# Two more steps of a top-k attention kernel transpose their weights on TensorE, and one pair is dealt fewer products

## The chip, the cores and the metric

The kernel runs on one core of one Trainium2 chip. The metric is device time in microseconds (us) of one execution, lower is better. The time before is the median of three executions, 1654.76 us (1654.59 to 1656.15). One further execution, taken by the hardware profiler, lasted 1655.26 us; its span from first to last instruction is 1653.4 us.

## What is computed

Attention that keeps the 32 largest scores of each row, then a low-rank token mixer and a two-layer channel network:

```python
# q, k, v: 8 batches x 8 heads x 576 rows x 64, float32
scores = scale * q @ k.T
kth    = 32nd largest of each row of scores
attn   = softmax(where(scores >= kth, scores, -1e9))
x      = (attn @ v), heads side by side          # 8 x 576 x 512
u      = x + (x.T @ U @ V).T                     # rank 32
out    = u + relu(u @ w_ch1) @ w_ch2             # 512 -> 2048 -> 512
```

## The kernel before

**Tiling.** Two heads form a *pair*, four pairs a batch: pairs 0 to 31, in the code `g`. The 576 rows of a pair are four tiles of 128 rows (t = 0 to 3) and a tail of 64 (t = 4, both heads in one tile). A *step* is one (g, t); from pair 4 on the tail goes together with t = 3, so a pair has four steps. The second batch is pairs 4 to 7, and its third pair is pair 6. The loop over steps is at the end of the kernel; step number n = 20 is (4, 0), n = 28 is (6, 0).

**What a step does.** TensorE makes the scores (L350, tail L382), ScalarE copies them out of PSUM (L395, tail L415 and L418). From pair 5 on, the two halves of a row are folded: GpSimd adds them (L446), VectorE takes their maximum (L448), GpSimd subtracts it (L449); then VectorE searches for the 32 largest with alternating MAX8 and MATCH_REPLACE8 (L500, L502, L521, L534, L539). L502 opens a step's search and needs L449. The threshold goes to ScalarE (L565, L571), GpSimd subtracts the gap (L572), ScalarE takes the exponential (L453). The resulting weights must be transposed before they can be multiplied with v (L708, L711, tail L682; copied out at L720).

**Two ways to transpose.** `turns` does it on TensorE: nine 128x128 transposes per step (L634 eight times, L639 once) into PSUM, through a ring of two buffers named tp, and three ScalarE copies into PT (L635 twice, L640). `blocks` does it on VectorE: three stream transposes of 32x32 blocks (L598) into y, four DMAs from SyncE's queue that write y to DRAM (L604), and later, in `back`, one DMA on ScalarE's queue that reads it all into PT (L613). `shared(g, t)` says which: when it is true, `blocks` is called at the end of the step's follower and `turns` returns at once. The tail always goes through TensorE.

**Products dealt between the steps.** The two layers of the previous batch's channel network are a generator of matmuls (L845 the first layer, L862 the second), called in small portions by `fill`, eight times a step. One unit is a matmul of 512 columns; a batch has 144 units, and a portion is 144/(4 x 8 x 4.4) = 1.023 units, times 1.4 in a pair's last step. In pairs 4 to 7 and the first three steps of pair 8 the portion is multiplied by EARLY, one factor a pair (the last one also in those three steps). What isn't done in time is done later: the next batch's network can't start before its input is complete, and waits (`yield 0`), in which case the portion lapses. Every engine takes its instructions in the order in which this loop has emitted them.

**Other names.** L750, L761, L773, L781, L785, L800 and L801 belong to the low-rank mixer (`mixed`), L873, L874, L886, L888 and L890 to the way of the network's output back to DRAM, L857 to the first layer's activation. VectorE's L320 transposes the next pair's q and k, which SyncE's queue loads (L272, L277). L938 is the last batch's network, with its own scheme. ACT is ScalarE, DVE VectorE, POOL GpSimd.

Of the kernel before, what the change touches and what calls it, by code (L numbers as in the profile page):

```python
# [26 lines left out]
def kernel(  # L27
# [35 lines left out]
    NT, TAIL = 4, 64  # L63
# [8 lines left out]
    ROUNDED = NPAIR + 2  # L72
# [512 lines left out]
    def shared(g, t):  # L585


        return t < NT and g >= ROUNDED

    def blocks(g, t):  # L590

# [26 lines left out]
    def turns(g, t):  # L618


        if shared(g, t):
            return
        E2 = probs.pop((g, t))
        nh = 2 if t < NT else 1
        if t == NT and g >= NPAIR:
            PT = attn.tile([P, NT + 1, P], F32, tag="PTt", name="PTt", bufs=1)
        else:
            PT = attn.tile([P, 2 * NT + 1, P], F32, tag="PT", name="PT")
        PTs[g, t] = PT
        for h in range(nh):  # L630
            tp = ps_t.tile([P, NT, P], F32, tag="tp", name="tp")
            for j in range(NT):
                a = h * (S + TAIL) + j * P
                nc.tensor.transpose(tp[:, j, :], E2[:, a : a + P], ident)  # L634
            nc.scalar.copy(PT[:, NT * h : NT * h + NT], tp)  # L635
            yield
        tp = ps_t.tile([P, P], F32, tag="tp", name="tp")
        a = MAIN if nh == 2 else S - P
        nc.tensor.transpose(tp, E2[:, a : a + P], ident)  # L639
        nc.scalar.copy(PT[:, NT * nh], tp)  # L640
        yield
# [31 lines left out]
    def values(g, t):  # L673
# [31 lines left out]
        if shared(g, t):  # L705
            PT = PT.rearrange("p c n -> p (c n)")
            PT = PT.rearrange("p (a c j) -> p c a j", a=4, j=BLK)
# [452 lines left out]
    BATCH = NPAIR * NT  # L1160


    SLOTS, LONG, EARLY = 8, 1.4, (1.1, 0.75, 0.91, 0.95)
    share = MLP_WORK / (NPAIR * SLOTS * (NT - 1 + LONG))
    fillers, mixing, due = [], [], 0.0

# [48 lines left out]
    t = 0  # L1215
# [5 lines left out]
    for n in range(STEPS + 2):  # L1221
        if n < STEPS:
            g, t = steps[n][0]
# [8 lines left out]
        else:  # L1232
            t = NT
# [109 lines left out]
        for tile_ in tiles(n - 1):  # L1343
            if shared(*tile_):
                blocks(*tile_)
# [50 lines left out]
```

## Time and profile before

| what | value |
|---|---|
| median of three runs | 1654.76 us |
| the profiled execution | 1655.26 us |
| its span | 1653.4 us |
| mean granted TensorE clock | 0.971 |
| L598, stream transpose of 128x512 | 208 times, 681 ns mean |
| L598, stream transpose of 128x128 | 104 times, 269 ns mean |
| L635, copy of 128x512 to PT | 52 times, 600 ns mean |
| L640, copy of 128x128 to PT | 28 times, 271 ns mean |
| L845 and L862, products | 1792 records each, two a matmul |

TensorE's ends are modelled, so that its busy share says little; starts are what counts, and a float32 product leaves two records. A time such as 312.86 is in us from the span's start. In a timeline a row gives start, duration, engine, line, operation, tiles and count, and in brackets the engine's idle time before it with what ended it. In a table of windows the columns are the stretch, its length, then the busy us and the instructions of TensorE, its weight loads, VectorE, ScalarE and GpSimd, the granted TensorE clock, the busy share of the DMA engines, and GB/s.

### The profile page before, as it was taken

What the parts mean: (1) busy time and instruction counts of PE and PEld (TensorE: products, weight loads), DVE (VectorE), ACT (ScalarE), POOL (GpSimd) and SP (SyncE); (2) the same over time, 40 slices, a digit from 0 to 9 for tenths busy, and PEclk for the clock granted to TensorE, in tenths of its full rate; (3) what the DMA queues carried; (4) which work ended last, traced back from release to release, by engine and by line L of the source; (5) the groups of instructions that cost most, each with busy time, mean ns of one, the idle gap of its engine ahead of it and who ended that gap; (6) DMA issues with size and microseconds to landing.
All of it is one profiled execution on the core that took longest, in us unless ns stands there. A gap on an engine that the chain in (4) does not pass through costs nothing.

```text
span 1653.4 us, 30246 instructions
## 1 busy us (share of the span) xinstructions
PE 1554.9 (94%) x9638; PEld 1182.0 (71%) x9638; DVE 1546.1 (94%) x4394; ACT 990.1 (60%) x2475; POOL 1009.4 (61%) x881
## 2 busy tenths in 40 slices
PE   4566799999899999999999999999999999999998
PEld 2344466787667877788777877788777877788776
DVE  7999999999999999999999999999999999994452
ACT  4888887665556556565656556565656656564320
POOL 4888768656566565656566565656566565653720
PEclk7787899999999999999999999999999999999999
DMA  3333331345445455554545455554545455543001
GB/s 89 102 96 99 88 88 31 84 128 139 132 120 142 127 141 136 143 139 129 134 123 143 125 146 134 143 139 127 135 123 144 126 148 134 139 123 108 7 2 28
DMA packets 280399, 189.42 MB, mean 115 GB/s; under 512 B 174288, under 2 KB 261168, under 8 KB 280240
## 3 DMA queue, kind: packets, MB, share of 16 engines
q1 hardware_dynamic: 259728, 117.62, 29.6%
q10 hardware_dynamic: 20512, 69.87, 13.3%
q8 instruction: 76, 1.25, 0.3%
q14 instruction: 83, 0.68, 0.1%
HBM read 116.49 MB, written 70.91 MB: 113 GB/s over the span
## 4 chain that ended last, share of the span: by engine, by line
PE 69%; DVE 22%; DMA 3%; POOL 2%; SPq 1%; ACT 1%; issue 1%; DVEq 0%; ACTq 0%; POOLq 0%
PE mm L862 21%; PE mm L845 20%; DVE m L539 7%; PE sc L350 6%; DVE upper L534 6%; PE O L711 6%; PE mm L938 3%; DVE first L521 2%; PE tp L938 2%; PE sc L938 2%; PE sc L382 2%; PE up L785 2%; DVE y L598 1%; PE O L708 1%; DVE upper L502 1%; DVE place L534 1%
## 5 line engine op out<-in xcount | busy, mean ns | idle before, releaser
L845 PE MATMUL mm<-uT,w 128*128 128x320 f32 (+1 forms) x1792 | 460.2, 408 | 2.1 <-POOL uT L801 2.1
L862 PE MATMUL mm<-hT,w 128*128 128x320 f32 (+1 forms) x1792 | 460.4, 407 | 0.0
L572 POOL TENSOR_TENSOR Ssb<-Ssb,E 128x576 f32<-128x576 f32 x243 | 339.7, 1417 | 196.9 <-ACT E L571 196.8
L845 PEld LDWEIGHTS mm<-uT,w 128*128 128x128 f32 x1792 | 333.3, 190 | 102.2 <-issue 10.0
L862 PEld LDWEIGHTS mm<-hT,w 128*128 128x128 f32 x1792 | 331.9, 190 | 91.7 <-issue 9.8
L539 DVE MAX8 m<-upper 128x8 f32<-128x304 f32 (+1 forms) x774 | 362.5, 509 | 0.7
L534 DVE MATCH_REPLACE8 upper<-m,upper 128x304 f32<-128x304 f32 (+1 forms) x516 | 256.6, 504 | 0.0
L446 POOL TENSOR_TENSOR lower<-Ssb 128x576 uint32<-128x576 uint32 x108 | 152.3, 1410 | 134.2 <-ACT Ssb L395 66.9
L449 POOL TENSOR_TENSOR lower<-lower,upper 128x576 uint32<-128x576 uint32 x108 | 152.3, 1410 | 123.6 <-DVE upper L448 119.7
L453 ACT ACTIVATE Ssb<-Ssb,nmax 128x576 f32<-128x576 f32 x258 | 201.8, 784 | 19.9 <-POOL Ssb L545 9.6
L350 PE MATMUL sc<-qkT 64*128 64x288 f32 (+1 forms) x1056 | 177.5, 457 | 9.6 <-ACT Ssb L404 8.5
L571 ACT ACTIVATE E<-Ssb,least 128x576 f32<-128x576 f32 x243 | 176.2, 768 | 4.2
L502 DVE MAX8 upper<-lower 128x8 f32<-128x288 f32 x432 | 171.8, 439 | 2.3 <-POOL lower L449 2.3
L395 ACT COPY Ssb<-sc 128x576 f32<-128x576 f32 x216 | 127.6, 642 | 73.5 <-PE sc L350 73.5
L598 DVE STREAM_TRANSPOSE y<-Ssb 128x512 f32<-128x512 f32 (+1 forms) x312 | 154.0, 544 | 0.4 <-ACT Ssb L453 0.4
L711 PE MATMUL O<-PT,va 128*64 128x128 f32 x2048 | 144.1, 284 | 0.0
L857 ACT ACTIVATE hT<-mm 128x320 f32<-128x320 f32 (+1 forms) x224 | 91.2, 407 | 85.0 <-PE mm L845 81.5
L350 PEld LDWEIGHTS sc<-qkT 64*128 64x128 f32 (+1 forms) x1056 | 95.2, 196 | 50.5 <-issue 18.9
L711 PEld LDWEIGHTS O<-PT,va 128*64 128x64 f32 x2048 | 112.6, 140 | 16.2 <-issue 1.6
L720 ACT COPY XT<-O 128x128 f32<-128x128 f32 x128 | 33.8, 264 | 114.3 <-PE O L711 107.3
L534 DVE MATCH_REPLACE8 upper<-first,upper 128x304 f32<-128x304 f32 x216 | 97.5, 459 | 0.0
L500 DVE MATCH_REPLACE8 lower<-upper,lower 128x288 f32<-128x288 f32 x216 | 93.9, 442 | 0.0
(268 smaller groups left out, 2261.1 us busy)
## 6 DMA issues: line engine op xcount, KB each, us to landing
away<-y SPq DMA_DIRECT2D x416, 144.0 KB
PT<-away ACTq DMA_DIRECT2D x104, 576.0 KB
raw<-in_moe_w_ch_dram SPq DMA_DIRECT2D x32, 512.0 KB
va<-in_v_dram SPq DMA_DIRECT2D x64, 128.0 KB
scale<-rd ACTq DMA_DIRECT2D x56, 144.0 KB
out_dram<-ob SPq DMA_DIRECT2D x59, 128.0 KB
ld<-in_q_dram SPq DMA_DIRECT2D x108, 64.0 KB
ld<-in_k_dram SPq DMA_DIRECT2D x108, 64.0 KB
```

Source lines behind the costliest of these rows:

```text
L350: nc.tensor.matmul(out, lhsT=qkT[half(h), 0, cols(t)], rhs=qkT[half(h), 1, lo:hi], start=True, stop=True,)
L446: nc.gpsimd.tensor_tensor(bottom, a.bitcast(U32), b.bitcast(U32), ALU.add)
L453: nc.scalar.activation(E, chunk, AF.Exp, bias=nmax, scale=SCALE, accum_out=total)
L502: nc.vector.max(spot, lower)
L534: nc.vector.match_replace(nxt, ms[c], curs[c], NEG)
L539: nc.vector.max(ms[c], curs[c])
L571: nc.scalar.activation(gap, chunk, AF.Relu, bias=least[:, c : c + 1], scale=-WIDEN)
L572: nc.gpsimd.tensor_tensor(chunk, chunk, gap, ALU.subtract)
L598: nc.vector.transpose(y[:, :, i * NT : i * NT + c].rearrange("p r c j -> p c r j"), E2[:, a : a + c * P].rearrange("p (c r j) -> p c r j", ...
L711: nc.tensor.matmul(O[half(h)], lhsT=va[:, h, j, :], rhs=PT[:, NT * h + j], start=False, stop=(j == NT - 1),)
L845: nc.tensor.matmul(phs[f][:, 0:w], lhsT=first_layer(cc, f), rhs=uT[:, cc, lo:hi], start=(cc == 0), stop=(cc == NC - 1),)
L862: nc.tensor.matmul(po[:, 0:w], lhsT=w2[:, f, c * P : (c + 1) * P], rhs=hTs[f][:, 0:w], start=(f == 0), stop=(f == NF - 1),)
```

## The change

The predicate now sends the first two steps of pair 6 to TensorE as well, and pair 6 is dealt fewer products, pair 7 and the three steps after it slightly more:

```diff
     def shared(g, t):
-        return t < NT and g >= ROUNDED
+        return t < NT and (g, t) >= (ROUNDED, NT // 2)
...
-    SLOTS, LONG, EARLY = 8, 1.4, (1.1, 0.75, 0.91, 0.95)
+    SLOTS, LONG, EARLY = 8, 1.4, (1.1, 0.75, 0.78, 0.97)
     share = MLP_WORK / (NPAIR * SLOTS * (NT - 1 + LONG))
```

ROUNDED is 6 and NT is 4, so the comparison starts at (6, 2). The places at which the loop asks `shared`, and the two functions it chooses between, are unchanged:

```python
        for tile_ in tiles(n - 1):
            if shared(*tile_):
                blocks(*tile_)
        turning = turned(n - 1)
...
    def turns(g, t):
        if shared(g, t):
            return
```

In the order in which the built program's instructions stand, L598 occurs 306 times after, 312 before; L634 336 times after, 320 before; L639 58 times after, 56 before; L845 and L862 896 times each in both. The orders differ from pair 6's first steps until the step that follows the scores of (8, 3), and are the same from there to the end.

## The prediction

> **What bounds the kernel now.** I read the page's busy shares and chain first, then windows, then the timelines of each engine around pair 6.
>
> ```profile
> PE 1554.9 (94%) x9638; PEld 1182.0 (71%) x9638; DVE 1546.1 (94%) x4394; ACT 990.1 (60%) x2475; POOL 1009.4 (61%) x881
> ...
> PE 69%; DVE 22%; DMA 3%; POOL 2%; SPq 1%; ACT 1%; issue 1%; DVEq 0%; ACTq 0%; POOLq 0%
> ```
>
> TensorE and VectorE are both nearly full, and the chain that ended last has both. Where it changes from one to the other decides this case. The windows:
>
> ```profile
> 294.00:341.00 47.00, 46.15 (x315) 36.23 (x311) 44.60 (x137) 30.39 (x81) 28.86 (x25) 1.00 0.32 85
> ...
> 388.00:435.00 47.00, 42.13 (x278) 31.13 (x276) 46.97 (x144) 27.27 (x69) 28.96 (x26) 0.96 0.50 136
> ...
> 575.00:761.40 186.40, 186.27 (x1190) 143.74 (x1189) 185.84 (x565) 112.25 (x285) 115.20 (x100) 1.00 0.51 135
> ```
>
> Pair 6 is the first row: VectorE lacks 2.4 us. In pair 8 VectorE never rests and TensorE lacks 4.9 us. One later batch, the third row, has TensorE full and VectorE with 0.56 us to spare; the next batch repeats it to the record count. So VectorE sets the time up to about 490 us, TensorE after it. The chain says the same: mostly VectorE and the DMAs behind its transposes until 491.10, then TensorE's products almost without a break until 1485. The point of change is a wait for a PT tile:
>
> ```profile
> 491.10 0.49 PE L708 MATMUL O<-PT,vd 128*128 128x128 f32 x2 [1.85 <-DMA PT<-away]
> ```
>
> From 297 to 575 TensorE waited this often:
>
> ```profile
> PE O L708 <- DMA PT<-away: 4.9, 4, 1.9
> PE mm L845 <- POOL uT L801: 2.1, 1, 2.1
> ```
>
> From 575 to 1480 the same query names no wait of TensorE at all. The waits also cost clock:
>
> ```profile
> 413.50:416.90 3.40, 1.70 (x9) 0.86 (x8) 3.40 (x11) 1.16 (x5) 2.41 (x5) 1.00 0.59 191
> 416.90:420.30 3.40, 3.37 (x30) 2.42 (x31) 3.40 (x7) 2.08 (x5) 2.17 (x3) 0.54 0.20 47
> 488.60:492.00 3.40, 1.55 (x13) 0.92 (x13) 3.37 (x12) 2.68 (x7) 2.31 (x3) 1.00 0.52 168
> 492.00:495.40 3.40, 3.40 (x22) 2.04 (x19) 3.40 (x14) 1.22 (x3) 1.88 (x2) 0.54 0.68 175
> ```
>
> After a stretch of 3.4 us in which TensorE was busy for half or less, the next one runs at about half clock: some 1.7 us of TensorE's work lost, twice, the second time on the path.
>
> **What the Trainium skill says.** "TensorE: Matmul & The Clock Gate", Part 1, describes this clock: a free-running window of 3.4 us, half rate after an idle one. The rows above agree, and free-running means that the loss may come or go between runs. Its Part 4 says that a TensorE transpose lands in PSUM and has to be copied out; the trace agrees (L635, L640). "VectorE: DVE Perf Modes", section "The three transpose paths", says that VectorE transposes 32x32 blocks only; here that shows as the detour y, DRAM, PT behind L598.
>
> **The change part by part.**
>
> *Removed from VectorE.* Three L598 for (6, 0) and three for (6, 1). From start to start they take 314.26 - 312.86 = 1.40 and 325.81 - 324.40 = 1.41, together 2.8 us.
>
> ```profile
> 312.86 1.48 DVE L598 STREAM_TRANSPOSE y<-Ssb 128x512 f32<-128x512 f32 x3
> 314.26 0.78 DVE L502 MAX8 upper<-lower 128x8 f32<-128x288 f32 x2
> ...
> 322.08 0.76 DVE L448 TENSOR_TENSOR upper<-sc,Ssb 128x576 f32<-128x576 f32 x1 [1.44 <-ACT Stail L415]
> ...
> 324.40 1.48 DVE L598 STREAM_TRANSPOSE y<-Ssb 128x512 f32<-128x512 f32 x3
> 325.81 1.34 DVE L320 STREAM_TRANSPOSE qkT<-ld 128x1152 f32<-128x1152 f32 x1
> ```
>
> What is late next: at the first place L502, which needs GpSimd's L449. That ran from 311.44 for 1.42, to 312.86, just when VectorE would arrive: a wait of 0 to 0.3, I take 0.05 (in the new order an L874 of 0.87 stands before L449, but L446 ahead of it can start earlier, as ScalarE's L571 no longer stands behind an L873 that waited 1.58 for TensorE). At the second, L320 still covers L449. Eight L604 and two L613 go too; SyncE's loads then stand behind two waits less, worth nothing here.
>
> *The stall at 322.08.* VectorE waited 1.44 for the scores of (6, 3). TensorE had started them (L350) at 319.68; L448 follows 2.4 later. With two products of 320 columns less before the scores of (6, 2) (0.54 each: sixteen records in 4.31) and one product and three L886 (0.33) less between them, these scores start about 1.9 earlier, at 317.8, and L448 can run at 320.2. VectorE would come at 320.64 - 1.35 = 319.3. About 0.9 of the 1.44 stays, 0.5 goes.
>
> *Added to TensorE.* 16 L634 and 2 L639. Their price:
>
> ```profile
> 308.20 1.09 PE L634 MATMUL tp<-ident,Ssb 128*128 128x128 f32 x8
> ```
>
> Eight start within 0.93 (the next product is at 309.13), four in 0.43 in the chain, so 0.11 each and 2.0 us in all. The first nine stand right after the scores of (6, 3), the others after those of (7, 0).
>
> *Dealt products.* Pair 6 loses 0.13 x 36 = 4.7 units; a unit is 0.54 x 512/320 = 0.86 us, so 4.0 us. Pair 7 gets 0.7 units, the three next steps 0.5. The rest, about 2 units, or four products of 256 columns by the new order, runs after the scores of (8, 3), where the portions lapsed before and where TensorE stood idle (408 to 425). It delays nothing there.
>
> *Added to ScalarE.* Two times L635, L635, L640: 0.60 + 0.60 + 0.27 = 1.47 each, 2.9 us on an engine busy for 30.4 of pair 6's 47. They stand in order before an L453. The tp ring has two buffers, and in the new order the first two copies come after L395, L415 and L418, so that an L886 on TensorE waits about 0.5; I take 0.5 for each step, bounds 0 and 1.5.
>
> *Does TensorE keep up?* Against before, the scores start: (6, 3) -1.9, (7, 0) -1.6, (7, 1) -1.2, (7, 2) -1.7 (a wait of 0.63 for L781 goes), (7, 3) -1.3. VectorE is then 2.8 + 0.5 - 0.1 = 3.2 early. The tightest place is (7, 3): ScalarE's copies ended at 366.35 and L448 ran at 368.56, 2.2 of slack, against 1.9 wanted. It just holds; a loss of 0 to 0.8 lies in the range. In pair 8 slack is 3.6 and more, and TensorE's waits there (1.1, 1.4, 0.2 and 2.1, by DMA and L801, which follow VectorE) let it catch up.
>
> *The sum.* VectorE, and with it the DMA that TensorE waits for at 491.10, comes 3.2 us earlier. From there on the order is unchanged and TensorE sets the time, so 3.2 carries to the end. In the likeliest case one more thing goes: TensorE reaches that place with less idle time, or at another phase of the clock's window, and the half-clock stretch at 492.0 or most of the DMA wait isn't met. The first is worth up to 1.7, the second up to 1.8; I take 1.4. VectorE can follow: it stood idle for 0.7 + 0.4 in pair 10 for this same delay, and rests 0.4 a batch later. Sum: 1655.26 - 3.2 - 1.4 = 1650.7. The profiled execution was 0.5 above the median; I compare the forecast with the median as it stands, 4.1 below it.
>
> **The rivals.**
>
> *A, the forecast:* 3.2 and a part of the wait or clock at 490, between 1648.9 (both whole) and 1651.4. Chance 0.57.
>
> *B, only VectorE's part arrives:* TensorE meets the same DMA wait and the same half clock 3 us earlier. For it: both follow VectorE. 1655.26 - 3.2 = 1652.1; with up to 1.3 lost at (7, 3) or 491, 1653.4. Chance 0.26, of which 0.04 ends beyond 0.2%.
>
> *C, nothing arrives:* the transposes' 2.0 us on TensorE aren't covered by idle time but shift the chain after 491, against 3.2 gained: 1654.1, up to 1655.5. Against it: 7.8 us of waits between 297 and 495. Chance 0.09.
>
> *D, slower:* TensorE falls behind in pair 6, because the tp ring is held by copies that stand in ScalarE's order behind waiting ones. If each of the four groups of eight and one waits 1.5 for its copy (6 us), less the 4.0 of products taken out, plus the 2.0 of transposes, TensorE is 4 later at pair 7; the slack there is 2 to 5, so VectorE waits instead of gaining, and a new half-clock window adds 1.7. It decides from about 6 us of ring waits on. 1658.7. Against it: pair 5 transposes all its steps so, and TensorE's waits around them from 250 to 298 add up to 2.2 (0.9, 0.7, 0.4 and 0.2). Chance 0.08.
>
> *That it doesn't do what it says* can be excluded: six L598 fewer, eighteen transposes more, equal products.
>
> **How the numbers follow.** 0.2% is 3.3 us, about what a measurement of this kernel can tell from no change. Faster by more: 0.57 + 0.04 = 0.61. Within: 0.22 + 0.09 = 0.31. Slower: 0.08. The range takes in A and B, 1648.9 to 1653.4, and leaves out C and D.
>
> **What would show it.** No L598 before (6, 2)'s at about 337; L448 of (6, 3) at about 320 with a wait near 0.9; the L502 after it at 323.8 instead of 327.06; VectorE without idle time in pairs 7 to 9; the L708 that started at 491.10 at 488 or earlier; the clock table without, or with, a half-clock stretch after it; batches of 186.4 as before. The prediction is wrong if VectorE stands idle in pair 7, or if TensorE's batches become longer.

## The result and the profile after

The changed kernel takes 1651.49 us (median of 14 runs, 1650.63 to 1654.33), the kernel before in the same comparison 1654.70 us (14 runs, 1653.91 to 1657.64). The ratio is 0.9979, with a 95% interval of 0.9971 to 0.9986: 3.2 us faster. A second comparison on the chip, further down, gives 0.9976 (0.9967 to 0.9984). The two intervals are gains of 2.3 to 4.8 us and 2.6 to 5.5 us. Of all executions timed for this study one, of the spare transposes further down, took 3139.16 us; the ratios leave it out. The forecast was 1650.7, the range 1648.9 to 1653.4.

The profiled execution of the changed kernel took 1653.27 us, more than its median. It lost that time before the change acts: VectorE opened (6, 0) at 296.84 us, not at 294.22 as before. Over all runs of this study that moment lies between 294.2 and 296.8. So I count from VectorE's first L502 of (6, 0) on. From that point to the opening of (9, 0), two executions of one kernel agree within 0.06 us.

First the page's engine row and the shares of its chain, for the changed kernel:

```profile
PE 1558.9 (94%) x9656; PEld 1185.5 (72%) x9656; DVE 1543.5 (93%) x4388; ACT 993.8 (60%) x2481; POOL 1009.1 (61%) x881
...
PE 72%; DVE 13%; POOL 5%; ACT 4%; DMA 2%; SPq 1%; issue 1%; DVEq 0%; ACTq 0%; POOLq 0%
```

Eighteen matmuls more on TensorE and six instructions fewer on VectorE, as the change says. VectorE's share of the chain has gone from 22% to 13%. That does not mean that VectorE is free now. The chain is one path among several of nearly the same length.

The timeline of VectorE in pair 6 shows where the time went:

```profile
306.49 0.82 DVE L502 MAX8 upper<-lower 128x8 f32<-128x288 f32 x2 [0.94 <-POOL lower L449]
...
315.50 0.82 DVE L502 MAX8 upper<-lower 128x8 f32<-128x288 f32 x2
...
322.96 0.76 DVE L448 TENSOR_TENSOR upper<-sc,Ssb 128x576 f32<-128x576 f32 x1 [1.03 <-ACT Stail L415]
...
326.57 0.78 DVE L502 MAX8 upper<-lower 128x8 f32<-128x288 f32 x2
...
340.00 1.48 DVE L598 STREAM_TRANSPOSE y<-Ssb 128x512 f32<-128x512 f32 x3
```

Before, the last two of these rows stood here:

```profile
327.06 0.78 DVE L502 MAX8 upper<-lower 128x8 f32<-128x288 f32 x2
...
340.49 1.48 DVE L598 STREAM_TRANSPOSE y<-Ssb 128x512 f32<-128x512 f32 x3
```

Subtract 2.62 from the rows of the changed kernel to compare with before. The search that began at 314.26 now begins at 312.88, the one at 327.06 at 323.95, and the L598 at 340.49 stands at 337.38. The L502 at 315.50 has no bracket (idle times under 0.15 us get none): GpSimd's L449 is in time. L448 still waits for the scores of (6, 3), for 1.03 us where it was 1.44.

On TensorE the added transposes follow the scores of (6, 3), and those of the next step follow the scores of (7, 0) (rows of the timeline, where one row merges neighbours of a kind):

```profile
320.56 1.24 PE L350 MATMUL sc<-qkT 64*128 64x288 f32 x8
321.74 0.66 PE L634 MATMUL tp<-ident,Ssb 128*128 128x128 f32 x4
322.23 0.71 PE L862 MATMUL mm<-hT,w 128*128 128x320 f32 x2
322.77 0.60 PE L634 MATMUL tp<-ident,Ssb 128*128 128x128 f32 x4
...
324.19 0.33 PE L639 MATMUL tp<-ident,Ssb 128*128 128x128 f32 x1
...
332.62 0.27 PE L761 MATMUL tp<-ident,uT 128*64 128x128 f32 x1 [0.35 <-ACT PT L635]
```

Of the brackets in pair 6, the last one, 0.35 us, is the only new one that a copy out of the tp ring causes. Then the waits of TensorE from 290 to 575 (us in total, times, longest):

```profile
PE mm L845 <- POOL uT L801: 2.1, 1, 2.1
PE tp L634 <- ACT XT L720: 0.9, 1, 0.9
PE O L708 <- DMA PT<-away: 0.6, 2, 0.3
```

The wait of L708 for the DMA was 4.9 and is 0.6. And the place that stood at 491.10, in the timeline, with the two windows of the clock around it below:

```profile
486.71 2.32 PE L862 MATMUL mm<-hT,w 128*128 128x320 f32 x8
488.94 0.49 PE L708 MATMUL O<-PT,vd 128*128 128x128 f32 x2
```

```profile
488.17:491.58 3.41, 3.41 (x31) 2.13 (x29) 3.38 (x12) 2.02 (x5) 2.18 (x2) 1.00 0.28 48
491.58:495.00 3.42, 3.42 (x20) 2.66 (x19) 3.42 (x13) 2.74 (x8) 3.15 (x3) 1.00 0.68 174
```

L708 does not wait, and TensorE's clock stays at 1.00. Counted from (6, 0) it comes at 192.10 instead of 196.88, so 4.8 us earlier.

This table counts from VectorE's first L502 of (6, 0) to that of the steps named; the last column runs to the end of the span:

| kernel | (7,0) | (9,0) | (11,0) | (20,0) | (31,3) | end |
|---|---|---|---|---|---|---|
| before | 47.68 | 140.60 | 234.85 | 653.90 | 1197.31 | 1359.22 |
| before, profiled again | 47.67 | 140.59 | 234.85 | 653.91 | 1197.30 | 1359.08 |
| changed | 44.57 | 137.50 | 230.43 | 648.62 | 1191.84 | 1354.65 |
| changed, profiled again | 44.56 | 137.49 | 230.42 | 648.59 | 1191.75 | 1354.25 |
| transposes alone | 47.72 | 140.65 | 233.58 | 651.84 | 1195.56 | 1357.99 |
| dealing alone | 46.13 | 139.05 | 231.99 | 650.69 | 1194.11 | 1355.91 |
| two later steps too | 44.56 | 137.49 | 230.43 | 649.92 | 1193.33 | 1355.61 |
| spare transposes | 47.67 | 140.60 | 233.53 | 651.72 | 1194.68 | 1357.41 |

The 4.57 us from (6, 0) to the end divide like this. Pair 6 gives 3.11. From (9, 0) to (11, 0) it took 94.25 and takes 92.93, which gives 1.32. From (11, 0) to the end it took 1124.37 and takes 1124.22: nothing more. VectorE's further lead of 1.05 at (31, 3) is gone at the end, to within the 0.7 us by which three profiled executions of the changed kernel differ there (1354.25 to 1354.96).

### The profile page after: what moved, and what is told of

Same layout as the page of the kernel before. It is cut to its first block, busy times and chain, and to the rows that moved or that the text cites. A ratio compares the mean times of both kernels' runs of the same rounds, so it can differ in the third digit from the quotient of the medians.

```text
span 1651.5 us, 30266 instructions
## 1 busy us (share of the span) xinstructions
PE 1558.9 (94%) x9656; PEld 1185.5 (72%) x9656; DVE 1543.5 (93%) x4388; ACT 993.8 (60%) x2481; POOL 1009.1 (61%) x881
## 4 chain that ended last, share of the span: by engine, by line
PE 72%; DVE 13%; POOL 5%; ACT 4%; DMA 2%; SPq 1%; issue 1%; DVEq 0%; ACTq 0%; POOLq 0%
PE mm L862 22%; PE mm L845 21%; PE sc L350 7%; PE O L711 6%; DVE m L539 4%; DVE upper L534 3%; PE mm L938 3%; PE up L785 2%; PE tp L938 2%; PE sc L938 2%; PE sc L382 2%; PE O L708 1%; PE tp L634 1%; DVE first L521 1%; DVE upper L502 1%; POOL E L544 1%
## 5 line engine op out<-in xcount | busy, mean ns | idle before, releaser
L845 PE MATMUL mm<-uT,w 128*128 128x320 f32 (+1 forms) x1792 | 461.1, 408 | 2.6 <-POOL uT L801 2.1
L862 PE MATMUL mm<-hT,w 128*128 128x320 f32 (+1 forms) x1792 | 460.6, 408 | 0.0
L845 PEld LDWEIGHTS mm<-uT,w 128*128 128x128 f32 x1792 | 333.1, 190 | 102.5 <-issue 9.6
L862 PEld LDWEIGHTS mm<-hT,w 128*128 128x128 f32 x1792 | 332.0, 190 | 91.6 <-issue 9.8
L449 POOL TENSOR_TENSOR lower<-lower,upper 128x576 uint32<-128x576 uint32 x108 | 152.4, 1411 | 135.9 <-DVE upper L448 134.0
L502 DVE MAX8 upper<-lower 128x8 f32<-128x288 f32 x432 | 171.8, 438 | 1.7 <-POOL lower L449 1.7
L395 ACT COPY Ssb<-sc 128x576 f32<-128x576 f32 x216 | 127.5, 642 | 72.7 <-PE sc L350 72.6
L598 DVE STREAM_TRANSPOSE y<-Ssb 128x512 f32<-128x512 f32 (+1 forms) x306 | 150.9, 543 | 0.0
```

The costliest lines, as they stand in the source:

```text
L449: nc.gpsimd.tensor_tensor(bottom, bottom, top.bitcast(U32), ALU.subtract)
L502: nc.vector.max(spot, lower)
L845: nc.tensor.matmul(phs[f][:, 0:w], lhsT=first_layer(cc, f), rhs=uT[:, cc, lo:hi], start=(cc == 0), stop=(cc == NC - 1),)
L862: nc.tensor.matmul(po[:, 0:w], lhsT=w2[:, f, c * P : (c + 1) * P], rhs=hTs[f][:, 0:w], start=(f == 0), stop=(f == NF - 1),)
```

## The experiments

**The two parts apart.** Theory: VectorE gains 2.8 us only if TensorE brings the scores earlier, which the smaller dealing does. Rival: one of the two edits is enough. The first kernel has the new predicate and the old dealing, the second the reverse:

```diff
-        return t < NT and g >= ROUNDED
+        return t < NT and (g, t) >= (ROUNDED, NT // 2)
```

> The kernel before with only the two steps' transposes moved to TensorE, the products dealt as before. Measured from VectorE's first L502 of (6, 0) to that of (9, 0): before 140.6 us, the changed kernel 137.5. Theory (both halves are needed): the first L598 that goes is swallowed by the wait for the scores of (6, 3), which grows from 1.44 to about 2.8, because no product was taken from ahead of those scores; of the second, TensorE's 2.0 us of transposes take most back at (7, 3), where slack is 2.2. The stretch is 139.2 to 140.6, the time 0 to 1.4 us under before. Rival (VectorE's work alone counts): 137.8, the time 2.8 under before.

```diff
-    SLOTS, LONG, EARLY = 8, 1.4, (1.1, 0.75, 0.91, 0.95)
+    SLOTS, LONG, EARLY = 8, 1.4, (1.1, 0.75, 0.78, 0.97)
```

> The kernel before with only the new factors 0.78 and 0.97, the transposes where they were. Theory: the wait of 1.44 for the scores of (6, 3) goes, nothing else in pair 6, so the same stretch is 139.2 instead of 140.6, and the time 1.4 us under before, more if the DMA wait at 491 is met in another way. Rival (the dealing is the whole gain, the transposes only move): 137.5 and 3.2 under before.

The transposes alone: 1653.57 us against 1654.40, ratio 0.9996 (0.9988 to 1.0004). The dealing alone: 1653.22 us, 0.9995 (0.9986 to 1.0003). At (9, 0), the first is 0.05 late, the second 1.55 early, both together 3.11 early. The timeline of VectorE in the first kernel shows what became of the six L598:

```profile
318.44 0.85 DVE L539 MAX8 m<-upper 128x8 f32<-128x304 f32 x2
322.05 0.76 DVE L448 TENSOR_TENSOR upper<-sc,Ssb 128x576 f32<-128x576 f32 x1 [2.76 <-ACT Stail L415]
...
327.04 0.82 DVE L502 MAX8 upper<-lower 128x8 f32<-128x288 f32 x2 [1.31 <-POOL lower L449]
```

L448 stands where it stood before (322.08): VectorE came 1.3 earlier and waited 1.3 longer for the scores of (6, 3). The second saving becomes a wait for L449, since L449 needs this L448. So both savings are eaten in pair 6 already. I had expected the second one to go later, at (7, 3). In the changed kernel the scores come earlier: L448 waits 1.03, and the L502 after it has no bracket. The dealing alone gains 1.55 in pair 6, which is about the stall of 1.44. The two parts are worth more together in pair 6 (3.11) than apart (-0.05 + 1.55), so the rival falls for either edit. The times agree as far as they go: neither part alone is clear of no change, the two together are. From (6, 0) to the end, the profiles show more, 1.2 and 3.3 us; 1.3 of each is the matter of pair 10, below.

**Two later steps on TensorE as well.** If TensorE sets the time after 491, the same exchange in pair 16 must cost what TensorE gets, although VectorE is relieved by 2.8 us there. The rival, that VectorE bounds there too, expects a gain.

```diff
-        return t < NT and (g, t) >= (ROUNDED, NT // 2)
+        return t < NT and (g, t) >= (ROUNDED, NT // 2) and (g, t) not in ((16, 0), (16, 1))
```

> The changed kernel with the transposes of (16, 0) and (16, 1) moved to TensorE as well, no product taken out for them. Theory (from about 490 us on TensorE sets the time, without idle time): 18 transposes of 0.11 us are added and the end comes 1 to 2 us later than in the changed kernel; VectorE's 2.8 us turn into idle time of VectorE at the scores of later steps. Rival (VectorE still sets the time there): 2.8 us earlier.

1652.83 us (21 runs), 0.9987 (0.9980 to 0.9994) against before; the changed kernel had 0.9979. From (6, 0), it equals the changed kernel until pair 14 (369.82 against 369.83), is 1.30 later at (20, 0), and 0.96 later at the end (0.65 to 1.36 later than the three profiled executions of the changed kernel). That is less than the 2.0 us that TensorE gets, and just under the 1 to 2 expected; what hides the rest was not traced. VectorE's waits from 250 to 1500, first in the changed kernel and then in this one:

```profile
DVE upper L502 <- POOL lower L449: 1.7, 2, 0.9
DVE upper L448 <- ACT Stail L415: 1.6, 3, 1.0
```

```profile
DVE upper L448 <- ACT Stail L415: 3.0, 5, 1.2
DVE upper L502 <- POOL lower L449: 2.7, 3, 1.0
DVE upper L448 <- ACT Ssb L395: 1.1, 1, 1.1
```

The sums are 3.3 and 6.8: VectorE waits for the scores and folds after them instead of transposing. The transposes alone cost 0.05 us in pair 6, where TensorE has idle time ahead of 491, and the same number of them cost 1.3 us at (20, 0), where it has none. That agrees with the prediction's reading of the windows. Whether fewer products in pair 16 would have changed this was not tried.

**What the 1.3 us at pair 10 are.** Before was profiled again, to see whether its wait at L708 comes back, and a kernel was made that leaves pairs 6 to 10 as before but puts 18 transposes of the identity at step 10, long ahead of them. It puts 18 more matmuls ahead of TensorE's later instructions and so moves the places at which TensorE fetches them. (The spare results go nowhere.)

> The kernel before, unchanged, with another profile. Theory: the start of (6, 0) on VectorE, 293.98 before and 296.60 in the changed kernel, differs between executions of one and the same code by 1 to 3 us, with the half-clock stretches of the first 200 us; the stretch from (6, 0) to (9, 0) is the same within 0.2 (140.6). The DMA wait near 491 and the half-clock stretch after it may or may not come. Rival (these belong to the program): 293.98 again, and both again.

```diff
+        if n == 10:
+            spare_ = ps_t.tile([P, P], F32, tag="tp", name="spare_")
+            for _ in range(18):
+                nc.tensor.transpose(spare_, ident, ident)
```

> The kernel before with 18 more TensorE transposes of the identity, early (step 10 of the loop, where TensorE is idle a third of the time), whose result nobody reads. It moves the places at which TensorE fetches its instructions (one 16 KB packet every 256 of its instructions) by as many instructions as the change does, and touches nothing in pairs 6 to 10. Theory: the wait near 491 comes from such a fetch that falls between the writes to away and the read of PT, 1.5 us of delay; shifted, the PT read is issued 5.5 to 6.0 us after its L598 instead of 7.0, TensorE's gap there is under 0.6 instead of 1.85 to 2.0, VectorE's idle 1.1 in pair 10 goes, and the stretch from the first L502 of (6, 0) to that of (11, 0) is 233.6 as with the transposes alone, instead of 234.85; (9, 0) stays at 140.6. Rival (the wait depends on how early VectorE or how busy TensorE is): 234.85, and the gap again.

> The changed kernel unchanged, with another profile. Theory: the start of (6, 0) lies near 294.4 as in the others and not at 296.84; from it to (9, 0) 137.5, to (11, 0) 230.4, to the end 1354.7, each within 0.3. Rival (the change itself delays the start): 296.8 again.

The single times were 1655.34 (before), 1653.73 (spare transposes) and 1651.39 (changed). Before again: the wait returns, 2.03 us, and so does the half clock after it. Changed again: neither. (6, 0) opened at 294.47 in before and at 295.34 in the changed kernel, so that the 296.84 of its first profile does not belong to it (294.4 had been expected). The spare transposes change nothing until (9, 0) (140.60 as before), and then gain the same 1.32 that the changed kernel gains: from (9, 0) to (11, 0) 92.93. So this part of the gain needs neither pair 6's transposes on TensorE nor its dealing: 18 idle matmuls, long before, do the same.

Its cause can be followed one step back. The trace of before holds 76 packets of 16 KB on a queue of kind "instruction" (and packets of 8 KB on another one, which I leave aside). "Runtime: NRT & Kernel Launch", section "Instruction fetch mechanics", says that each engine fetches its instructions over DMA in blocks of 16 KiB, 256 instructions. The trace agrees for TensorE: from one packet of 16 KB to the next, some 20 us, it records 256 instructions of TensorE on average. In before, one came at 189.9 us from (6, 0), between the last write of L604 (issued at 188.5) and the read L613 (192.7), which needs those writes. With the spare transposes it came at 186.9, ahead of the writes, and in the changed kernel at 183.9, also ahead of them. From the first L598 to the issue of L613 it took 486.92 - 479.89 = 7.03 us in before, 484.93 - 479.40 = 5.53 in the changed kernel (before's two rows come first):

```profile
479.89 1.48 DVE L598 STREAM_TRANSPOSE y<-Ssb 128x512 f32<-128x512 f32 x3
486.92 0.33 ACTq L613 DMA_DIRECT2D PT<-away  x1
```

```profile
479.40 1.48 DVE L598 STREAM_TRANSPOSE y<-Ssb 128x512 f32<-128x512 f32 x3
484.93 0.35 ACTq L613 DMA_DIRECT2D PT<-away  x1
485.33 0.42 ACT L873 COPY oT<-mm 128x320 f32<-128x320 f32 x1 [1.48 <-DMA away<-y]
```

The spare transposes had 6.10, the transposes alone (fetch at 187.5, after the first of their writes) 6.00, the dealing alone, whose fetch at 188.4 fell behind its writes (185.6 to 187.0), 7.1. These agree with a fetch that delays the writes by some 1 to 1.5 us. Two other steps show the same in the kept traces. At (15, 2) a packet falls between the last write and the read in both executions of before and in the dealing alone, 6.88 to 6.99 us from transpose to read; in the ten other executions it doesn't, 5.28 to 5.33. At (9, 0) it is the other way round: the two executions of before have none there, 5.18 and 5.20, and the two of the spare transposes do, 6.72 and 6.95. At later steps the difference is often smaller or absent. No run isolates the fetch from all else that 18 more matmuls shift, so its part remains a reading, though a supported one.

The longer wait alone is not what costs 1.3, and this was not what I had thought. The dealing-alone kernel waits too, for 1.62 us (its timeline), yet it needs 92.94 from (9, 0) to (11, 0), as the changed kernel does. The windows of the clock tell the difference. First before's window that holds the wait and the one after it, then the same for the dealing alone:

```profile
488.85:492.26 3.41, 1.56 (x18) 1.04 (x18) 3.38 (x10) 2.43 (x7) 2.32 (x2) 1.00 0.48 152
492.26:495.68 3.42, 3.42 (x20) 2.06 (x15) 3.42 (x14) 1.50 (x3) 1.62 (x2) 0.50 0.67 172
```

```profile
490.01 0.49 PE L708 MATMUL O<-PT,vd 128*128 128x128 f32 x2 [1.62 <-DMA PT<-away]
```

```profile
487.67:491.08 3.41, 1.79 (x17) 1.14 (x17) 3.38 (x12) 2.69 (x7) 2.41 (x3) 1.00 0.62 169
491.08:494.50 3.42, 3.42 (x28) 2.40 (x24) 3.42 (x13) 2.11 (x5) 2.73 (x3) 1.00 0.68 174
```

TensorE was busy for 1.56 of 3.41 in before and ran at half clock next; in the other kernel it was busy for 1.79 and kept its full clock. Before profiled again had 1.38 and half clock. So the 1.3 us belong to the half-clock stretch, and the wait counts when it empties about half of one window.

**Does that part show in the times?** Three kernels were timed in one comparison: the spare transposes, the changed kernel, and the variant described next.

> The kernel before with the 18 early spare transposes, timed. Theory: the place of TensorE's instruction fetch is worth 1 to 1.7 us at the end in most executions, so the median is 1 to 1.7 us under before although no work was removed; the rest of the changed kernel's gain, 1.5 to 2.5 us, is the transposes and the dealing. Rival (the wait near 491 is rare or costs nothing in most executions): the median of before, within 0.4 us.

> The changed kernel, timed beside the others. Theory: 3.0 to 3.6 us under before; from (6, 0) to (9, 0) 137.5 again.

Before: 1654.74. The changed kernel: 1651.07, ratio 0.9976 (0.9967 to 0.9984). The spare transposes: 1654.29, ratio 1.0000 (0.9992 to 1.0008), so the 1 to 1.7 us that I expected did not show, although their profiled execution was again at 233.77 for (11, 0), about 1.1 better than before. The interval reaches 1.3 us to either side, so a small gain is possible but not shown. An estimate says why it may be small: a wait of 1.85 leaves 1.7 or more idle inside one window of 3.41 in (3.41 - 1.85 + 2 x 0.15) / 3.41 = 54% of the phases, if all phases are alike. Both profiled executions of before met it; about half of the timed ones would not, which leaves some 0.7 us on average. Whether they did can't be read from times.

**Going on in the same direction.** The changed kernel still waits 1.03 at the scores of (6, 3). With 0.70 in place of 0.78, still fewer products stand ahead of them; the second variant also moves a third step, (6, 2), to TensorE.

```diff
-    SLOTS, LONG, EARLY = 8, 1.4, (1.1, 0.75, 0.78, 0.97)
+    SLOTS, LONG, EARLY = 8, 1.4, (1.1, 0.75, 0.70, 0.97)
```

> The changed kernel with the third factor 0.70 instead of 0.78. Theory: the wait of 1.03 for the scores of (6, 3) goes with 2.9 units less in pair 6, the wait of 0.94 at (6, 1) stays, so (9, 0) is 136.5 after (6, 0) instead of 137.5; what is owed runs after the scores of (8, 3) still. At the end TensorE is the bound and part of it is lost: 0 to 1 us under the changed kernel. Rival (TensorE then owes too much and VectorE waits in pair 7 or 8): later than the changed kernel.

> The changed kernel with the third factor 0.70, timed beside the others. Theory: 0.5 to 1 us under the changed kernel. Rival: no difference to it, the earlier 1650.33 was the session.

```diff
-        return t < NT and (g, t) >= (ROUNDED, NT // 2)
+        return t < NT and (g, t) >= (ROUNDED, NT - 1)
```

> Three steps of pair 6 through TensorE, and the third factor 0.70. Theory: VectorE saves another 1.4 us, (9, 0) is 135.1 to 136.0 after (6, 0), but TensorE, with 1.0 us more and nothing idle after 490, gives at most a part of it at the end: 0 to 1 us under the changed kernel. Rival (VectorE sets the end): 2.4 under the changed kernel.

| kernel | median us | ratio to before | (7,0) | (9,0) | end |
|---|---|---|---|---|---|
| 0.70 | 1650.33 | 0.9975 (0.9965 to 0.9984) | 43.88 | 136.80 | 1354.03 |
| 0.70, timed again | 1650.25 | 0.9977 (0.9967 to 0.9987) | 43.90 | 136.83 | 1354.27 |
| 0.70, three steps | 1650.20 | 0.9969 (0.9957 to 0.9981) | 42.49 | 136.34 | 1354.63 |

With 0.70, the wait of 1.03 is gone, but one of 0.40 for L449 has come at (6, 2): (7, 0) comes 0.69 earlier than in the changed kernel, and the lead holds at (9, 0), which had been expected at 136.5. The third step gives another 1.39 at (7, 0), of which 0.93 is gone at (9, 0), since VectorE waits on the way (0.80 at L448 of (7, 3)). The 135.1 to 136.0 expected for it at (9, 0) were missed. At the end all three lie within the spread of the changed kernel's three profiled executions (1354.25 to 1354.96) or a little under it. The medians are 0.8 to 1.3 us below the changed kernel's, but the intervals of the ratios overlap: 0.70 is the better setting by the profile, by an amount that these runs don't establish.

## Why the prediction was right, step by step

- *Removed from VectorE, 2.8.* Right. The opening of (6, 2)'s search, the L502 at 315.50, moved by 314.26 - 312.88 = 1.38. The next one moved by 3.11 in all. A new wait at the first L502 is too short to be listed (1.38 came of 1.40); 0.05 was taken.
- *The stall at 322.08, 0.5.* Right in kind, nearly in size: 1.03 stays where 0.9 was expected, so 0.41 went. The transposes alone show how much hung on it: without the earlier scores nothing of the 2.8 arrives.
- *TensorE's transposes, 2.0, and ScalarE's copies.* The cover held. No L886 waited for the ring; 0.35 at one L761 is the only new wait for it, where 0.5 a step was taken. Rival D, whose price was 6 us of ring waits, has no support.
- *Does TensorE keep up?* Yes, barely, and the prediction read its slack of 2.2 wrongly. It counted to the end of L395, at 366.35, but L448 waits for the copy after it: its bracket in pair 6 names L415. In before L415 ended at 366.24 + 0.50 = 366.74, and L448 ran at 368.56. The slack was 1.8, less than the 1.9 wanted, so 0.1 should have been lost. In the changed kernel L415 ended at 367.92 and L448 ran at 368.07, 0.15 later. It held by luck: the copies came 1.4 earlier against (6, 0), not 1.3, and VectorE 3.1, not 3.2. VectorE has no idle stretch of 0.15 us or more in pairs 7 to 13.
- *3.2 early in total.* 3.11 in pair 6. Right.
- *One more thing goes at 491, 1.4.* In the profiled executions it went: 1.32 between (9, 0) and (11, 0). That was luck. The prediction named less idle time of TensorE or another phase of the window as reasons; the spare transposes lose the wait without any change in pairs 6 to 9, by shifting TensorE's instructions. And the prediction took the 1.4 whole, although it says itself that the loss may come or go between runs and had seen one execution of before. The timed spare transposes show at most part of it.
- *The sum.* It starts from the profiled 1655.26, which is 0.56 above the median before, and this hides part of the 1.4 that was too much: the forecast misses 1651.49 by 0.8. Counted from the median, B's 3.2 gives 1651.5, just what was measured, and A's 4.6 gives 1650.1. The gains of the two comparisons, 3.2 and 3.7 us, have intervals that hold both. So the profile shows A, the medians lie at B or a little beyond, and the times cannot tell the two apart. The 3.1 us of pair 6 are what came for the reason given.
- *After 491 TensorE sets the time.* Right: 1124.37 and 1124.22 us from (11, 0) to the end, and the two later steps cost 0.96. A batch in the changed kernel, the columns as before:

```profile
575.00:761.40 186.40, 186.27 (x1192) 143.60 (x1190) 186.26 (x566) 112.99 (x287) 115.62 (x101) 1.00 0.51 136
```

Rival C, nothing arriving because the added 2.0 us shift the chain, is refuted by the same numbers: TensorE had the idle time ahead of 491 to absorb them.

Four smaller things in the prediction don't come out. Of the 4.7 units taken from pair 6 it places 0.7 + 0.5 + 2 = 3.2. In the traces 4.5 units go before the scores of (7, 1); 0.5 come back up to those of (8, 1), 2.0 from there to the scores of (8, 3), and 2.0 after. VectorE is not idle there, so it cost nothing. With both losses whole, A's lower end is 1655.26 - 3.2 - 1.7 - 1.8 = 1648.6, not 1648.9. How D comes to 1658.7 is not worked out. And the clock rows do not agree with a half rate after an idle window, as the prediction says they do: TensorE was busy for 1.70 and 1.55 us in the windows before.

## What to carry to other kernels

When you move work between two nearly full engines, look for a stretch where the receiver has idle time, and ask whether the next thing the relieved engine waits for comes earlier too. In this kernel the transposes alone gained nothing in their pair, the dealing alone 1.55 us, and both together 3.11; where TensorE had no idle time, the same number of transposes made the end later. Count such a gain from a fixed event near the change, not from the start of the span, since the stage before can differ by nearly as much as the gain (here 2.6 us of 3.1). A loss that hangs on the phase of the clock's window, and that one profile shows, should enter a forecast of a median with its chance, not whole.

## What the runs showed of the hardware

**Half clock after a half-idle window.** The records of half clock start at multiples of 3.41 us from each other in every run. "TensorE: Matmul & The Clock Gate", Part 1, puts the half rate after at least one idle window. Here less suffices, and the measurement decides. In thirteen profiled executions, from 205 to 1640 us of the span, I added up TensorE's busy time in each window. Seven windows were followed by half clock; they held between 1.03 and 1.72 us of work. Of all windows with 1.79 or more, none was. One with 1.65 us, right after a half-clock window, was not either. So the limit lies near half of the window, with that exception.

**A half-clock stretch can be free.** In before one fell at 417.2; in before profiled again there was none there, and VectorE opened (10, 0) at 187.07 from (6, 0) in both. In the spare-transposes kernel one fell at 418.9, again with 187.07: TensorE had slack in that stretch. At 491 such a stretch cost 1.3, for it left VectorE idle for 0.70 and 0.38 us in pair 10.

**A transfer that meets an instruction fetch can be late.** The trace counts the 16 KB packets of instructions among the traffic of the core's DMA engines. Where one fell between writes and the read that needs them, transpose to read took 7.0 to 7.1 us at pair 9, against 5.5 to 6.1 where it came earlier, and 6.9 to 7.0 against 5.3 at (15, 2). At other steps the difference is smaller or absent.
